# A fused attention, experts and gated layer: load order of q and k, the planner's durations, and the softmax factors spread before they are turned

## The chip, the cores and the metric

The kernel runs on one core of one Trainium2 chip. The metric is device time in microseconds (us); the time before is 1050.41 us, the median of three runs (1049.84 to 1050.56). The core's engines are TensorE (matrix products and transposes), VectorE, ScalarE, GpSimd, and SyncE, which issues most of the DMA transfers. Each runs its own instructions in order and waits for the others on semaphores.

## What is computed

The reference chains an attention, a mixture of experts and a gated layer, all in float32. The change lies in the attention (B, H, S, D = 4, 8, 576, 64):

```python
scores = scale * np.matmul(q, k.transpose(0, 1, 3, 2))
scores = np.where(causal, -1000000000.0, scores)
scores = scores - scores.max(-1, keepdims=True)
a = np.exp(scores)
a /= a.sum(-1, keepdims=True) + 1e-09
local = np.matmul(a, v)
# phi(x) = where(x > 0, x, exp(x) - 1) + 1
mem_out = np.einsum('bhsd,bhde->bhse', q_p, M_prev) / (np.einsum('bhsd,bhd->bhs', q_p, z_prev)[..., None] + 1e-06)
g = 1.0 / (1.0 + np.exp(-beta))[None, :, None, None]
return (g * mem_out + (1 - g) * local).astype(np.float32)
```

Here q_p is phi(q). The result, 2304 tokens of 512 numbers, goes through eight experts (each token to its best one) and then through `(sigmoid(x @ w_gate) * (x @ w_val)) @ w_out`.

## The kernel before

The attention works on 16 pairs of heads; a group is two pairs, so there are eight groups. For a group, SyncE loads q and k (`load_nat`, L230) in two halves l = 0, 1 of two heads each: two DMAs of 128 KB, and one of 32 KB for the last 64 rows. `load_z` (L246) loads z copied to all partitions in six DMAs, `load_M` (L262) M in two, `load_v` (L270) v in five. A pair's first three blocks of q and k need one half, its last two blocks both.

A pair then goes through these steps. TensorE turns q and k (`turn`, L322); ScalarE copies the high part of each and VectorE the low part (`q_part`, `z_part`, `k_part`); TensorE multiplies (`scores`, L391); VectorE adds the mask and finds each row's extreme (`masked`, L411); ScalarE takes the exponential and sums the rows (`exp`, L434); TensorE turns the probabilities (`turn_probs`, L475), ScalarE or VectorE keeps them (`keep_probs`), and TensorE multiplies with v (`out_part`, L504). GpSimd computes phi in four passes and a scaling (`phi_sum`, L286; `phi_scale`, L307), with the reduction between them on VectorE (`phi_norm`, L299). VectorE scales the product and adds the memory's part (`out_scale`, L519; `out_add`, L526).

The product with v comes out with the tokens along the free dimension, so a row's factor, (1 - g) over its sum, must be turned too and stand 64 times below itself. Before, `recip` (L441) makes nine factors per partition on VectorE, splits each into a high and a low part and writes these 18 columns into a table of 128 x 128; `rc_turn` (L451) transposes the table on TensorE, `rc_copy` (L455) brings it to SBUF, and `fan` (L458) multiplies it with six selection matrices of zeros and ones (`choices`, L210), four times for 128 columns and twice for the last 64; `fan_copy` (L471) takes the result to `rb`.

The order of all this is the work of a planner, `Plan` (L57). Each step has a rank, a cost in us for each engine that may do it, the steps that it needs and the buffers that it takes. `Plan.order` runs a list of ready steps forward in time by these costs and by a lag from engine to engine, and the program is written in the order found. The steps of the attention are entered in `Attention.run` (L533): `("L", "q", gi, l)` is a half of q, `("phs", gi, n)` a pass of phi, `("r", pi)` the factors, `("rt", pi)` and `("rk", pi)` their transposition and copy, `("b", pi, bk)` and `("bc", pi, bk)` the two parts of `fan` and `fan_copy`. The hardware then runs each engine's instructions in that order, whatever they take.

Of the kernel before, what the change touches and what calls it, by code (L numbers as in the profile page):

```python
# [56 lines left out]
class Plan:  # L57
# [7 lines left out]
    LAG = {"PE": 0.2, "SP": 2.2, "PL": 0.15, "DV": 0.2, "AC": 0.17, "Q": 0.0}  # L65
    SAME = {"PE": 0.0, "DV": 0.13, "PL": 0.1, "AC": 0.06, "SP": 0.0, "Q": 0.0}
# [16 lines left out]
    def order(self):  # L83
# [17 lines left out]
        while ready:  # L101
            best = None
            for n in ready:
# [4 lines left out]
                for e, c in cost.items():  # L108
                    t = max([free.get(e, 0.0), *t0, *(end[m][0] + (self.SAME if end[m][1] == e and (e != "SP" or n[0] == "ld") else self.LAG)[end[m][1]] for m in needs)])
# [24 lines left out]
class Attention:  # L134
# [14 lines left out]
    def constants(self, beta):  # L149
# [5 lines left out]
        self.rcs = [cp.tile([P, P], F32, name=f"rc{i}") for i in range(2)]  # L155
        self.rT = cp.tile([P, P], F32R, name="rT")
# [32 lines left out]
        for c in range(4):  # L189
            nc.vector.tensor_copy(self.iog[:, :, 2 * c : 2 * c + 2], o2)  # L190
        for j in range(2):
            r = slice(j * 64, (j + 1) * 64)
            nc.vector.tensor_copy(self.iog[r, :, 8:9], o2[r, :, j : j + 1])
# [16 lines left out]
    def choices(self):  # L210

        nc, cp, n = self.nc, self.cp, 2 * NQ
        whole = self.pt[1].rearrange("p h k q -> p (h k q)")[:, 0 : 6 * P].rearrange("p (c m) -> p c m", m=P)
        nc.gpsimd.memset(whole, 0.0)
        f = whole[0:n]
        fill = dict(compare_op=ALU.not_equal, fill=1.0, channel_multiplier=1)
        for part in range(2):
            for c in range(4):
                v = f[:, c].rearrange("p (j d) -> p j d", j=2)
                nc.gpsimd.affine_select(out=v, in_=v, pattern=[[-1, 2], [0, 64]], base=-NQ * part - 2 * c, **fill)  # L220
            for j in range(2):
                v = f[:, 4 + j, j * 64 : (j + 1) * 64]
                nc.gpsimd.affine_select(out=v, in_=v, pattern=[[0, 64]], base=-NQ * part - 8, **fill)
        self.pick = cp.tile([P, 6, P], F32R, name="pick")
        nc.gpsimd.tensor_copy(self.pick, whole)
        for rc in self.rcs:
            nc.gpsimd.memset(rc, 0.0)


    def load_nat(self, gi, nm, l):  # L230
# [6 lines left out]
        for hh in (2 * l, 2 * l + 1):  # L237
            self.nc.sync.dma_start(
                out=tv[:, :, hh, :], in_=src[b, h0 + hh, 0:512, :].rearrange("(c p) d -> p c d", p=P)
            )  # L240
        self.nc.sync.dma_start(
# [192 lines left out]
    def exp(self, pi, n):  # L434
# [3 lines left out]
            accum_out=self.sums[pi][:, n : n + 1],  # L438
# [12 lines left out]
    def rc_turn(self, pi):  # L451
        self.TR[pi] = T = self.ps_t.tile([P, 512], F32, name="T", tag="T")
        self.nc.tensor.transpose(T[:, 0:P], self.rcs[pi % 2], self.ident)

    def rc_copy(self, eng, pi):  # L455
        self.copy(eng, self.rT, self.TR[pi][:, 0:P])

    def fan(self, pi, bk):  # L458

        self.TR[pi, bk] = T = self.ps_t.tile([P, 512], F32, name="T", tag="T")  # L460
        r = self.rT
# [71 lines left out]
    def run(self, ex, change):  # L533
# [13 lines left out]
        def ac(n):  # L547
            return 0.06 + n / 1200
# [1176 lines left out]
```

## Time and profile before

| what | value |
|---|---|
| median of three runs | 1050.41 us |
| profiled execution | 1047.03 us |
| its span in the trace | 1045.3 us |
| TensorE (PE), busy share of the span | 95% |
| TensorE weight loads (PEld) | 82% |
| VectorE (DVE) | 52% |
| ScalarE (ACT) | 44% |
| GpSimd (POOL) | 21% |
| mean DMA rate | 100 GB/s |

The attention ends at about 270 us of the span, the experts' first product starts at 287.7, and the rest belongs to the experts and the gated layer. A share over the whole span says little about the attention, so its stretches have to be asked for apart. In the rows below a name such as `Sp<-kz,qT` is output and inputs, L399 a line of the kernel, x12 a count of instructions that are merged into one row, and the bracket gives how long the engine stood idle before and what ended it. SPq is SyncE's DMA queue, an issue's time is that of the issuing instruction and not of the transfer. Instructions of TensorE overlap in the array, so the distance from one start to the next is what counts there.

### The profile page before, as it was taken

To read this page: it belongs to the slowest core of one execution; us is meant where nothing else is said; L and a number is where in the kernel's file an instruction comes from. 1 tells how busy PE (TensorE), PEld (TensorE's weight loads), DVE (VectorE), ACT (ScalarE), POOL (GpSimd) and SP (SyncE) were. 2 spreads that over 40 slices of the span, in tenths; PEclk is the share of its full clock that TensorE was granted. 3 is DMA by queue.
4 is the path that set the end of the run, shared out by engine and by line. 5 is a ranking of instruction groups with operands and counts; after the bars stand their busy time and mean duration, and the time that the engine had idled before them with its cause. 6 is when DMAs were issued, how large, how long until landed. Compare 5 with 4: busy or idle time off the path is not lost. (4 is left out here: it accounts for less than half of the span.)

```text
span 1045.3 us, 18514 instructions
## 1 busy us (share of the span) xinstructions
PE 997.2 (95%) x5868; PEld 858.8 (82%) x5868; DVE 544.5 (52%) x1324; ACT 454.8 (44%) x1046; POOL 214.3 (21%) x344
## 2 busy tenths in 40 slices
PE   3989999899799999999999999999999999999997
PEld 3667777777688788888888999998999999999996
DVE  5897876777683853394466699912121121121111
ACT  3978786777542632282254555412221221122111
POOL 8785565332221111011011000001100100000001
PEclk9999999999999999999999999999999999999999
DMA  6756545430292661195247565300100100100000
GB/s 126 126 115 178 112 85 126 92 89 22 71 364 74 224 218 62 52 310 159 68 152 254 165 203 174 106 1 31 61 2 1 61 1 1 61 1 11 21 1 31
DMA packets 114851, 104.76 MB, mean 100 GB/s; under 512 B 71664, under 2 KB 89072, under 8 KB 114736
## 3 DMA queue, kind: packets, MB, share of 16 engines
q1 hardware_dynamic: 111264, 92.11, 30.9%
q0 software_dynamic: 3472, 11.30, 3.3%
q8 instruction: 49, 0.80, 0.3%
q14 instruction: 66, 0.54, 0.2%
HBM read 87.89 MB, written 15.50 MB: 99 GB/s over the span
## 5 line engine op out<-in xcount | busy, mean ns | idle before, releaser
L1532 DVE TENSOR_TENSOR G<-G,pT 128x384 f32<-128x384 f32 (+1 forms) x74 | 40.1, 542 | 247.6 <-PE pT L1518 239.6
L1564 POOL DMA_INDIRECT out_dram<-yo,rows x18 | 17.8, 991 | 453.5 <-ACT yo L1560 362.2
L1539 ACT ACTIVATE Gh<-G 128x384 fp32r<-128x384 f32 (+1 forms) x74 | 38.1, 516 | 158.2 <-DVE G L1532 158.0
L1313 PE MATMUL pY<-W,xh 128*128 128x512 f32 x368 | 98.0, 398 | 0.1
L1292 PE MATMUL pH<-W,xh 128*128 128x512 f32 x368 | 96.5, 394 | 0.7 <-ACT xh L1240 0.7
L1528 ACT ACTIVATE G<-pH 128x384 f32<-128x384 f32 x72 | 35.4, 491 | 121.0 <-PE pH L1518 120.6
L436 ACT ACTIVATE Sm<-Sm,mx 128x512 f32<-128x512 f32 (+3 forms) x144 | 83.6, 585 | 8.7 <-DVE mx L428 8.4
L1292 PEld LDWEIGHTS pH<-W,xh 128*128 128x128 f32 x368 | 69.6, 189 | 16.4 <-ACT xh L1240 1.0
L1313 PEld LDWEIGHTS pY<-W,xh 128*128 128x128 f32 x368 | 67.1, 188 | 13.5 <-ACT xh L1306 0.6
L1190 DVE TENSOR_TENSOR W<-raw,W 128x1024 fp32r<-128x1024 f32 x60 | 71.2, 1217 | 4.5 <-ACT W L1183 3.9
L428 DVE CUSTOM_DVE_ANT_0 Sm<-Sp,mask 128x512 f32<-128x512 f32 (+3 forms) x144 | 64.7, 482 | 15.9 <-PE T L480 6.9
L1306 ACT ACTIVATE xh<-pT 128x512 fp32r<-128x512 f32 x46 | 27.5, 598 | 101.9 <-PE pT L1232 91.8
L480 PE MATMUL T<-ident,Sm 128*128 128x128 f32 x400 | 62.2, 284 | 8.0 <-DVE xT L524 2.7
L1297 DVE TENSOR_SCALAR h<-pH 128x512 f32<-128x512 f32 x46 | 31.6, 687 | 72.0 <-PE pH L1292 71.1
L318 ACT ACTIVATE pt<-T 128x512 f32<-128x512 f32 (+4 forms) x138 | 56.0, 446 | 29.2 <-PE T L480 27.9
L480 PEld LDWEIGHTS T<-ident,Sm 128*128 128x128 f32 x400 | 44.8, 143 | 21.3 <-DVE xT L524 4.4
L1183 ACT ACTIVATE W<-raw 128x1024 fp32r<-128x1024 f32 x60 | 59.4, 1053 | 3.4 <-DVE xT L524 2.9
L1537 DVE TENSOR_TENSOR Gl<-G,Gh 128x384 fp32r<-128x384 f32 (+1 forms) x74 | 40.4, 545 | 32.7 <-ACT Gh L1539 32.7
L1292 PE MATMUL pH<-W,xl 128*128 128x512 f32 x184 | 56.3, 408 | 0.0
L1277 POOL DMA_INDIRECT xn<-x_dram,kept x23 | 25.5, 1110 | 149.2 <-DVEq L1359 86.4
L1313 PE MATMUL pY<-W,xl 128*128 128x512 f32 x184 | 49.9, 393 | 1.3 <-DVE xl L1304 1.3
L1304 DVE TENSOR_TENSOR xl<-pT,xh 128x512 fp32r<-128x512 f32 x46 | 31.7, 688 | 36.6 <-ACT xh L1306 30.7
(358 smaller groups left out, 2244.9 us busy)
## 6 DMA issues: line engine op xcount, KB each, us to landing
raw<-in_moe_w_dram SPq DMA_DIRECT2D x68, 512.0 KB, 5.9
y_dram<-y SPq DMA_DIRECT2D x23, 256.5 KB, 3.5
vn<-in_v_dram SPq DMA_DIRECT2D x40, 128.0 KB, 2.8
raw<-in_moe_w_gate_dram SPq DMA_DIRECT2D x10, 512.0 KB, 3.7
raw<-in_moe_w_val_dram SPq DMA_DIRECT2D x10, 512.0 KB, 3.8
raw<-in_moe_w_out_dram SPq DMA_DIRECT2D x10, 512.0 KB, 3.6
qn<-in_q_dram SPq DMA_DIRECT2D x32, 128.0 KB, 2.9
kn<-in_k_dram SPq DMA_DIRECT2D x32, 128.0 KB, 3.1
```

The lines of the kernel that those rows point to most:

```text
L318: self.nc.scalar.activation(out, in_, AF.Copy)
L428: self.nc.vector.tensor_tensor_reduce(out=self.Sm[pi, n][:, k0:k1], in0=self.Sp[pi, c][:, j if n < 8 else si, 0 : k1 - k0], in1=mask, scal ...
L436: self.nc.scalar.activation(self.Sm[pi, n], self.Sm[pi, n], AF.Exp, scale=-1.0, bias=self.mx[pi, n][:, si : si + 1], accum_out=self.sums[p ...
L480: nc.tensor.transpose(T[:, o * 128 : (o + 1) * 128], self.Sm[pi, n][:, k0 : k0 + 128], self.ident)
L1183: self.nc.scalar.activation(self.hi_lo(n)[0], self.first[n] if n in self.first else self.raw[n], AF.Copy)
L1190: eng.tensor_tensor(lo[:, o : o + w], t[:, o : o + w], hi.bitcast(F32)[:, o : o + w], ALU.subtract)
L1292: nc.tensor.matmul(pH[n], lhsT=a[:, m % 4, :], rhs=self.W1[:, c : c + 512], start=(m == 0), stop=(m == 11))
L1313: nc.tensor.matmul(pY[s % 2], lhsT=a[n][:, k * P : (k + 1) * P], rhs=self.W2[:, c : c + 512], start=(n == 0 and m == 0), stop=(n == 1 and ...
L1528: nc.scalar.activation(G[g, f][0], pp[g, f, 0], AF.Sigmoid)
L1532: nc.vector.tensor_tensor(t, t, p, ALU.mult)
L1537: nc.vector.tensor_tensor(l, t, hi.bitcast(F32), ALU.subtract)
L1539: nc.scalar.activation(hi, t, AF.Copy)
```

## The change

Four things change in the attention; the experts and the gated layer stay as they are.

1. Loads. `z`, `M` and `v` get later ranks, so both halves of q stand ahead of them. The first group's k is issued by ScalarE's own queue (a new engine name `AQ` in the planner), and its issues stand in ScalarE's program. The two small loads of the gate weights move from `Routing.constants` into a step of their own behind the first v.
2. Durations. The planner's costs for SyncE's issues, GpSimd's passes of phi and a few others are replaced.
3. Factors. `recip` keeps the nine factors, without a split, and makes two more columns of the first of them (the last 64 tokens, one column for each head of the pair). `spread` writes each of ten columns 64 times side by side into a tile of 128 x 640, on ScalarE or VectorE as the planner finds. `fan` transposes four blocks of it on TensorE, and multiplies the fifth with `fold`, two identity matrices one below the other, which adds its two halves.
4. The selection matrices, the table and its copy go, and their steps with them.

```diff
-    LAG = {"PE": 0.2, "SP": 2.2, "PL": 0.15, "DV": 0.2, "AC": 0.17, "Q": 0.0}
+    LAG = {"PE": 0.2, "SP": 2.2, "PL": 0.15, "DV": 0.2, "AC": 0.17, "AQ": 2.2, "Q": 0.0}
...
+        self.wides = [cp.tile([P, 5 * P], F32, name=f"wide{i}") for i in range(2)]
+        self.fold = cp.tile([P, 64], F32, name="fold")
+        nc.vector.tensor_tensor(self.fold, self.ident[:, 0:64], self.ident[:, 64:128], ALU.add)
+        self.head = cp.tile([P, 2], F32, name="head")
...
-    def load_nat(self, gi, nm, l):
+    def load_nat(self, eng, gi, nm, l):
+        queue = self.nc.scalar if eng == "AQ" else self.nc.sync
...
-        rc = self.rcs[pi % 2]
-        t = self.sp.tile([P, NQ], F32, name="rs", tag="rs", bufs=2)
-        nc.vector.scalar_tensor_tensor(t, self.sums[pi], 1e-9, self.iog[:, hp], ALU.add, ALU.mult)
-        nc.vector.reciprocal(t, t)
-        nc.vector.tensor_copy(rc.bitcast(F32R)[:, 0:NQ], t)
-        nc.vector.tensor_tensor(rc[:, NQ : 2 * NQ], t, rc[:, 0:NQ], ALU.subtract)
-
-    def rc_turn(self, pi):
...
+        self.rs[pi] = t = self.sp.tile([P, NQ + 2], F32, name="rs", tag="rs", bufs=2)
+        nc.vector.scalar_tensor_tensor(t[:, 0:NQ], self.sums[pi], 1e-9, self.iog[:, hp], ALU.add, ALU.mult)
+        nc.vector.reciprocal(t[:, 0:NQ], t[:, 0:NQ])
+        nc.vector.tensor_scalar(t[:, NQ:], self.head, t[:, 0:1], None, ALU.mult)
+
+    def spread(self, eng, pi):
+
+        self.wide[pi] = w = self.wides[pi % 2]
+        n = NQ + 1
+        self.copy(eng, w.rearrange("p (n d) -> p n d", d=64), self.rs[pi][:, 1:, None].to_broadcast([P, n, 64]))
...
         for n in range(3) if bk == 0 else (3,):
             o = (n - 3 * bk) * P
-            self.nc.tensor.matmul(T[:, o : o + P], lhsT=self.pick[:, n], rhs=r, start=True, stop=True, skip_group_check=True)
-        for j in range(2 * bk):
+            self.nc.tensor.transpose(T[:, o : o + P], w[:, n * P : (n + 1) * P], self.ident)
+        if bk:
             self.nc.tensor.matmul(
-                T[:, P : P + 64], lhsT=self.pick[:, 4 + j], rhs=r[:, j * 64 : (j + 1) * 64],
-                start=(j == 0), stop=(j == 1), skip_group_check=True,
+                T[:, P : P + 64], lhsT=w[:, 4 * P :], rhs=self.fold, start=True, stop=True, skip_group_check=True
             )
...
-                    add(("L", nm, gi, l), r + 2 * l + i, {"SP": 1.6}, lambda e, a=(gi, nm, l): self.load_nat(*a),
+                    add(("L", nm, gi, l), r + 2 * l + i, {"AQ" if (gi, nm) == (0, "k") else "SP": 1.9}, lambda e, a=(gi, nm, l): self.load_nat(e, *a),
...
-            add(("L", "z", gi), r + 2, {"SP": 2.7}, lambda e, g=gi: self.load_z(g), takes=[("zf", gi)])
+            add(("L", "z", gi), r + 3.5, {"SP": 3.3}, lambda e, g=gi: self.load_z(g), takes=[("zf", gi)])
...
-            for n, c in enumerate((3.06, 3.06, 2.57, 2.57)):
+            for n, c in enumerate((3.6, 3.6, 3.06, 3.06)):
```

What the planner makes of it, at three places. The first is the start on SyncE and on ScalarE (`qn`, `kn`, `zf`, `MB`, `vn` are the tiles of q, k, z, M and v; `wg` the gate weights). SyncE before:

```order
L238 DMA qn<-in_q_dram 128x4x64 x2
L241 DMA qn<-in_q_dram 64x2x64
L238 DMA kn<-in_k_dram 128x4x64 x2
L241 DMA kn<-in_k_dram 64x2x64
L251 DMA zf<-in_z_prev_dram 128x256 x4
L253 DMA zf<-in_z_prev_dram 64x128 x2
L238 DMA qn<-in_q_dram 128x4x64 x2
L241 DMA qn<-in_q_dram 64x2x64
L265 DMA MB<-in_M_prev_dram 64x2x64 x2
L747 DMA wg<-in_moe_w_gate_dram 128x4x8
L748 DMA wg<-in_moe_w_output_gate_dram 128x4x8
L238 DMA kn<-in_k_dram 128x4x64 x2
```

SyncE now; the last three rows belong to the second group:

```order
L224 DMA qn<-in_q_dram 128x4x64 x2
L227 DMA qn<-in_q_dram 64x2x64
L224 DMA qn<-in_q_dram 128x4x64 x2
L227 DMA qn<-in_q_dram 64x2x64
L237 DMA zf<-in_z_prev_dram 128x256 x4
L239 DMA zf<-in_z_prev_dram 64x128 x2
L251 DMA MB<-in_M_prev_dram 64x2x64 x2
L260 DMA vn<-in_v_dram 128x4x64 x4
L263 DMA vn<-in_v_dram 128x4x64
L224 DMA qn<-in_q_dram 128x4x64 x2
L227 DMA qn<-in_q_dram 64x2x64
L224 DMA kn<-in_k_dram 128x4x64 x2
```

ScalarE now, where k's issues surround the table load and the exponential of beta (`bt`):

```order
L224 DMA kn<-in_k_dram 128x4x64 x2
L227 DMA kn<-in_k_dram 64x2x64
L224 DMA kn<-in_k_dram 128x4x64
L186 ACT_TABLE_LOAD
L186 ACTIVATE bt<-bt 128x8
L224 DMA kn<-in_k_dram 128x4x64
L227 DMA kn<-in_k_dram 64x2x64
L340 ACTIVATE qT_117<-T 128x384
L362 ACTIVATE kz<-T 128x384
L270 ACTIVATE e<-qn 128x1152
```

The second half of q moved ahead of z, all of the first k moved to the other queue, and the second group's q moved behind v. The second place is VectorE at the factors of the ninth pair (`rs` the factors, `rc` the table, `rb` the turned factors). Before:

```order
L320 CAST rT<-T 128x128
L320 COPY rb<-T 128x192
L374 TENSOR_TENSOR kz<-T,kz 128x384
L446 SCALAR_TENSOR_TENSOR rs<-sums,iog 128x9
L447 RECIPROCAL rs<-rs 128x9
L448 CAST rc_109<-rs 128x9
L449 TENSOR_TENSOR rc_109<-rs,rc_109 128x9
L524 TENSOR_TENSOR xT<-O,rb 128x384
```

and now:

```order
L431 SCALAR_TENSOR_TENSOR rs<-sums,iog 128x9
L432 RECIPROCAL rs<-rs 128x9
L433 TENSOR_SCALAR rs<-head,rs 128x2
L306 COPY pt_159<-T 64x2x64
L306 COPY wide_109<-rs 128x640
L414 ISA Sm,mx<-Sp,mask 128x384
```

The two small operations and the copy of the turned table are gone, and the 640 columns of `wide` stand ahead of the next masked maximum. The third is TensorE at the factors of the last pair but one. Before:

```order
L406 MATMUL Sp<-kz,z_115 128x288 x6
L480 MATMUL T<-ident,Sm 128x128 x7
L453 MATMUL T<-ident,rc_109 128x128
L464 MATMUL T<-rT,pick 128x128 x4
L466 MATMUL T<-rT,pick 128x64 x2
L514 MATMUL O<-pt_154,vn 64x384 x2
```

and now:

```order
L447 MATMUL T<-ident,wide_109 128x128 x3
L316 MATMUL T<-ident,ph 128x128 x4
L320 MATMUL T<-ident,ph 128x128
L462 MATMUL T<-ident,Sm 128x128 x3
L392 MATMUL Sp<-kz,z_120 128x288 x6
L462 MATMUL T<-ident,Sm 128x128 x3
L447 MATMUL T<-ident,wide_109 128x128
L449 MATMUL T<-fold,wide_109 128x64
```

The first three blocks of the factors moved ahead of the last pair's last score products, and no table is turned before them.

## Rows read from the trace of the kernel before

**Rows 1.** Stretch; busy us of PE, PEld, DVE, ACT, POOL; granted clock, DMA share, GB/s.
```profile
0.00:270.50 270.50, 238.58 (x1955) 182.41 (x1959) 200.13 (x731) 198.09 (x628) 148.93 (x246) 0.99 0.49 104
35.00:40.00 5.00, 4.40 (x35) 3.61 (x35) 4.51 (x20) 5.00 (x18) 5.00 (x8) 1.00 0.81 68
180.00:190.00 10.00, 8.09 (x55) 6.38 (x51) 7.39 (x26) 6.37 (x21) 5.05 (x8) 0.83 0.42 52
```

**Rows 2.** Timeline of SyncE's DMA issues: start us, us, queue, line, operation.
```profile
0.74 0.98 SPq L238 DMA_DIRECT2D qn<-in_q_dram  x2
...
4.39 2.02 SPq L251 DMA_DIRECT2D zf<-in_z_prev_dram  x4
...
7.63 1.14 SPq L238 DMA_DIRECT2D qn<-in_q_dram  x2
...
10.43 2.61 SPq L265 DMA_DIRECT2D MB<-in_M_prev_dram  x2
...
14.87 1.05 SPq L238 DMA_DIRECT2D kn<-in_k_dram  x2
15.97 0.61 SPq L241 DMA_DIRECT2D kn<-in_k_dram  x1
...
19.45 1.05 SPq L238 DMA_DIRECT2D qn<-in_q_dram  x2
```

**Rows 3.** Timeline of TensorE, first 34 us; in brackets idle before and its end.
```profile
15.84 0.45 PE L334 MATMUL T<-ident,qn 128*128 128x128 f32 x1 [9.01 <-DMA qn<-in_q_dram]
...
18.51 0.48 PE L334 MATMUL T<-ident,kn 128*128 128x128 f32 x1 [0.95 <-DMA kn<-in_k_dram]
...
19.99 2.09 PE L399 MATMUL Sp<-kz,qT 64*128 64x512 f32 x12
...
26.48 0.49 PE L330 MATMUL T<-ident,qn 128*128 128x128 f32 x3
```

**Rows 4.** DMA issues of the first 30 us: count, KB each, median us to landing.
```profile
zf<-in_z_prev_dram SPq DMA_DIRECT2D x4, 128.0 KB, 6.1
```

**Rows 5.** Waits of SyncE's queue, first 60 us: us in total, times, longest.
```profile
SPq L265 <- DMA zf<-in_z_prev_dram: 2.3, 2, 1.4
```

**Rows 6.** Waits of the whole run: us in total, times, longest.
```profile
DVE nm L302 <- POOL e L297: 4.0, 2, 2.6
```

**Rows 7.** Timeline of ScalarE, first 34 us.
```profile
4.34 0.21 ACT L181 ACTIVATE bt<-bt 128x8 f32<-128x8 f32 x1 [2.32 <-DMA bt<-in_beta_dram]
```

**Rows 8.** Timeline of TensorE around one pair's factors.
```profile
44.16 0.77 PE L480 MATMUL T<-ident,Sm 128*128 128x128 f32 x5
44.68 0.64 PE L464 MATMUL T<-rT,pick 128*128 128x128 f32 x4
...
45.44 1.84 PE L514 MATMUL O<-pt,vn 128*64 128x384 f32 x16
```

**Rows 9.** Timeline of TensorE: f32 products of the logits.
```profile
271.94 1.18 PE L890 MATMUL T<-sel,LT 128*128 128x16 f32 x10
```

**Rows 10.** One line's instructions: ns min/median/max, first and last start, forms.
```profile
L446 DVE SCALAR_TENSOR_TENSOR rs<-sums,iog x16: 158/172/2410, 29.7 to 259.7; 128x9 f32<-128x9 f32 x16
```

**Rows 11.** VectorE's groups by shape, from 290 to 577 us: busy us, mean ns.
```profile
L1209 DVE TENSOR_SCALAR cv_a<-cv_a 128x512 f32<-128x512 f32 x6 | 2.5, 423 | 0.8 <-DVEq L1382 0.8
```

**Rows 12.** Timeline from 64.5 us: GpSimd, VectorE and TensorE.
```profile
65.13 3.06 POOL L297 TENSOR_TENSOR e<-ph,zf 128x320 f32<-128x320 f32 x4
...
65.80 2.41 DVE L446 SCALAR_TENSOR_TENSOR rs<-sums,iog 128x9 f32<-128x9 f32 x1
...
69.51 0.33 PE L480 MATMUL T<-ident,Sm 128*128 128x128 f32 x1 [1.09 <-DVE xT L524]
```

**Rows 13.** Timeline from 178 us: VectorE and TensorE.
```profile
182.54 1.35 DVE L302 TENSOR_REDUCE nm<-e 128x18 f32<-128x1152 f32 x1 [1.37 <-POOL e L297]
...
185.23 0.30 PE L330 MATMUL T<-ident,ph 128*128 128x128 f32 x1 [1.91 <-DVE xT L530]
...
185.70 1.91 PE L480 MATMUL T<-ident,Sm 128*128 128x128 f32 x8
```

More of the change, by code (lines that the diff above doesn't have):

```diff
@@ L108, in order @@
                 for e, c in cost.items():
-                    t = max([free.get(e, 0.0), *t0, *(end[m][0] + (self.SAME if end[m][1] == e and (e != "SP" or n[0] == "ld") else self.LAG)[end[m][1]] for m in needs)])
+                    t = max([free.get(e, 0.0), *t0, *(end[m][0] + (self.SAME if end[m][1] == e and (e != "SP" or n[0] in ("ld", "L")) else self.LAG)[end[m][1]] for m in needs)])
                     b_ = self.later.get(e, 0.0) if len(cost) > 1 else 0.0
@@ L637, in run @@
             r = u0 + 20
-            add(("r", pi), r, {"DV": 0.7}, lambda e, a=pi: self.recip(a), needs=[("e", pi, n) for n in range(NQ)] + ["pick"],
+            add(("r", pi), r, {"DV": 0.55}, lambda e, a=pi: self.recip(a), needs=[("e", pi, n) for n in range(NQ)],
                 takes=[("rc", pi)], uses=[("sums", pi)])
-            add(("rt", pi), r, {"PE": 0.15}, lambda e, a=pi: self.rc_turn(a), needs=[("r", pi)], takes=[("T", ("rt", pi))], uses=[("rc", pi)])
-            add(("rk", pi), r, {"AC": ac(128), "DV": dv(128)}, lambda e, a=pi: self.rc_copy(e, a), needs=[("rt", pi)], takes=[("rT", pi)], uses=[("T", ("rt", pi))])
+            add(("rw", pi), r, {"AC": ac(5 * P), "DV": dv(5 * P)}, lambda e, a=pi: self.spread(e, a), needs=[("r", pi)], takes=[("wd", pi)], uses=[("rc", pi)])
             for bk in range(2):
                 r, n = u0 + 21 + bk, QB[bk][1] - QB[bk][0]
-                add(("b", pi, bk), r, {"PE": PO + 0.33}, lambda e, a=(pi, bk): self.fan(*a), needs=[("rk", pi), "pick"] + ([("b", pi, 0)] if bk else []),
-                    takes=[("T", ("b", pi, bk))], uses=[("rT", pi)])
+                add(("b", pi, bk), r, {"PE": PO + (0.22 if bk else 0.3)}, lambda e, a=(pi, bk): self.fan(*a), needs=[("rw", pi)] + ([("b", pi, 0)] if bk else []),
+                    takes=[("T", ("b", pi, bk))], uses=[("wd", pi)])
                 add(("bc", pi, bk), r, {"AC": ac(n), "DV": dv(n)}, lambda e, a=(pi, bk): self.fan_copy(e, *a),
@@ L681, in run @@
             add(("k", n), 15 + n, {"PL": c}, lambda e: next(steps), needs=[("k", n - 1)] * (n > 0))
+        add("wg", 20, {"SP": 0.9}, lambda e: self.routing.load_gates(), needs=[("k", 0), ("L", "v", 0)])
         for b in range(B):
             self.routing.plan(self, add, b)
-        wide = [n for n in p.steps if n[0] in ("phn", "qh", "ql", "zh", "zl", "S", "m", "r", "rt", "rk", "b", "bc", "t", "v", "o", "os")]
+        wide = [n for n in p.steps if n[0] in ("phn", "qh", "ql", "zh", "zl", "S", "m", "r", "b", "bc", "t", "v", "o", "os")]
         for n in range(8):
@@ L803, in constants, with load_gates @@
         yield
+    def load_gates(self):
+        for i, w in enumerate(self.w_gates):
+            self.nc.sync.dma_start(out=self.wg[:, :, i * 8 : i * 8 + 8], in_=w.rearrange("(k p) e -> p k e", p=P))
     def cols(self, b):
@@ L813, in plan @@
         for bk in range(2):
-            add(("lg", b, bk), r, {"PE": 0.6}, lambda e, a=(at, b, bk): self.logits(*a), needs=xs[bk::2] + ([("lg", b, 0)] if bk else [("k", 4)]),
+            add(("lg", b, bk), r, {"PE": 0.6}, lambda e, a=(at, b, bk): self.logits(*a), needs=xs[bk::2] + ([("lg", b, 0)] if bk else [("k", 4), "wg"]),
                 takes=[("T", ("lg", b, bk))], uses=[("xT", b)], mode=3)
```

60 lines of the change are left out of this document (18 added, 42 removed).

## The prediction

> **What bounds the kernel now.** I read the busy time by stretch first, since the program is three stages in a row. The attention fills the first 270.5 us, and TensorE is busy 238.58 us of them [rows 1]; behind it come the experts and the gated layer, which the diff does not touch. So the change is worth what it takes off the attention, where TensorE does nothing for about 32 us. Where these lie is the next question. The DMA issues and the first uses show the largest piece: SyncE issues the first half of q and of k, then z, then the second half of q, and the second half of k only at 14.87 us [rows 2]. TensorE waits 9.01 us for the second half of q, until 15.84, and again for k until 18.51, and the first score products start at 19.99 [rows 3]. z is what holds the queue up: each of its large transfers takes 6.1 us to land, where the second k half is there 18.51 - 16.58 = 1.9 us after its last issue ended (15.97 + 0.61), and SyncE waits for z before it can issue M [rows 2 to 5]. Next come the engines behind the scores: from 35 to 40 us ScalarE is busy 5.00 of 5 us and VectorE 4.51 [rows 1], so the ramp is theirs rather than TensorE's. The last views are the waits and the timeline around a later gap. There VectorE, which runs in program order, stands before a reduction that needs GpSimd's product, twice in all, 4.0 us together [rows 6]; behind it are the additions that free accumulators.
>
> **The start: q and k before z, k on ScalarE's queue.** A half of q or k is three issues, and the second k half took SyncE 16.58 - 14.87 = 1.7 us for them [rows 2]. Two halves of q back to back, from 0.74, end at 4.2. On ScalarE four of k's six issues go out by about 3.0 at the same rate; then come the table load and the exponential of beta, which ended at 4.55 before [rows 7], and behind it the last two k issues, to about 5.7. That ScalarE waits for beta there delays nothing else, since its first copy needs a transposed q. With 1.9 us to landing k is whole at 7.6. But z is now issued from 4.2 on the other queue, beside k's last two transfers, and z's own 6.1 us is the other end: 5.7 + 6.1 = 11.8. I take 9.5, nearer the low end because only two of the six transfers meet z. From k's arrival to the first scores it took 19.99 - 18.51 = 1.5 us; now the second q half's exponential and the first blocks of the second pair stand in between, so I take 2.2. **Scores then start at 11.7 instead of 19.99: 8.3 us earlier** (10.2 at the low end, 6.0 at the high end).
>
> A rule of the Trainium skill speaks against the second queue. "DMA: Bandwidth & Descriptors", section "Issuing engines are not separate DMA queues", says that DMAs started by different engines run on the same sixteen DMA engines and interleave, and that a second issuer only saves issue time. No row here has a transfer that ScalarE started. On one queue the four halves would be issued by 0.74 + 4 x 1.7 = 7.5 and landed by 9.5, the value taken above, so by that rule the order of the loads is worth the 8.3 and the queue nothing.
>
> Who is late next: the loads of the second group. SyncE issued its first q at 19.45, and TensorE used it at 26.48 [rows 2, 3], 6.5 us after the first scores. Now z, M and v stand ahead of it. z's six issues take 3.2 us (4.39 to 7.63), so they end at 7.4 and z has landed at 13.5; M and v are held by it as M was, whose two issues took 2.6 us, and some 2 us of both lie behind that. So the issue comes at about 15.5, only 4 us earlier than before, and has landed 1.7 + 1.9 later, at 19.1. TensorE would be there at 11.7 + 6.5 = 18.2. I charge 1.0, and 0 to 3.5 as bounds (nothing, if ScalarE is behind by then anyway; the whole difference between 8.3 and 4 us with what hangs on it). **Term A: -8.3 + 1.0 = -7.3 us** (-10.2 to -2.5). The gate weights go behind v; they are first read by the logits, far later. GpSimd no longer builds the selection matrices; phi is first transposed long after the first scores, so I cost this at 0. If its chain came late, the pairs' last additions would wait, not the scores.
>
> **The softmax factors on TensorE.** Per pair it did one transpose of the factor table, four products against selection matrices and two more for the last 64 columns. From the first product to the next work is 45.44 - 44.68 = 0.76 us, and a transpose is (44.68 - 44.16) / 5 = 0.104, so 0.86 in all [rows 8]. Now it does four transposes, 0.42, and one product in full f32 with 64 columns. The nearest row to that is the logits' f32 product with 16 columns, ten instructions in 1.18 us, two to a product: 0.24 [rows 9]. So 0.66 us, and **term B is 16 x (0.66 - 0.86) = -3.2 us**. Ends: -3.6; and with 0.12 for a transpose and 0.36 for the product 16 x (0.84 - 0.86) = -0.3. It counts nearly in full, as TensorE is the busy engine after the ramp.
>
> **The same on VectorE and ScalarE.** Of the chain's small nine-column operations, 0.17 us in the median [rows 10], two go (cast and subtraction) and one comes (the last block's two columns); the copy of the turned table goes, eight times on each engine. What comes is the spread: 640 columns from SBUF to SBUF, twelve times on VectorE and four on ScalarE in the new order. The nearest row is a 512-column VectorE operation from SBUF to SBUF, 423 ns [rows 11], so 0.53 for 640; as the other end 1.1, as the spread reads each input 64 times and no row shows such a read. New on VectorE is 12 x 0.53 + 16 x 0.17 = 9.1 us, and 32 x 0.17 = 5.4 and eight copies go: near 0 in sum. But the spread is one long piece in VectorE's order, and masked maxima that TensorE needs queue behind it. On the other side the chain has two engine changes less. I charge **term D: +1.0 us** (-1 to +4).
>
> **Measured durations in the planner.** It sorts all steps by estimated times. GpSimd's product of phi with z was entered at 2.57 us; four pieces of it take 3.06 [rows 12]. So VectorE's reduction stood too early: at 182.54 VectorE had waited 1.37 us for GpSimd, TensorE stood idle for 1.91 until 185.23, and then eight transposes took 1.91 us, 0.24 each instead of 0.104 [rows 8, 13]; the granted clock of that stretch is 0.83 [rows 1], so part of it ran at 1.2 GHz. That is 1.9 + 8 x 0.136 = 3.0 us and some more until the clock was back, say 3.8. The other such wait, of 2.6 us, falls into the ramp, where ScalarE has a queue; I count 1. If the order now places the reductions right, 4.8 us go. SyncE's costs rise too, which moves prefetches that have slack. But a new order also makes collisions that the old trace can't show, so I take half: **term C: -2.4 us** (-4.8 to 0).
>
> **Sum.** -7.3 - 3.2 + 1.0 - 2.4 = -11.9 us on the profiled execution's own 1047.03 (span 1045.3 and 1.7 around it): 1035.1. The median of the runs shown is 1050.41, 3.4 above that execution, so the forecast is 1050.4 - 11.9 = **1038.5 us**.
>
> **Rivals.** First, the gain is given back in the ramp: the late loads and the full ScalarE hold the scores, so that half of A stays, and the new order misses as often as the old (C = 0): -3.6 - 3.2 + 1.0 = -5.8, 1044.6. For it: ScalarE's 5.00 of 5 us and SyncE's waits for z. Against it: ScalarE's queue there is filled by what TensorE gives it, which all comes earlier. Second, everything goes right, A without the late loads, all of C, no charge for the spread: -8.3 - 3.6 - 4.8 = -16.7, 1033.7. Third, k's last transfers are shuffled among z's packets and land at 11.8, scores at 14.0: A is -6.0 + 1.0 = -5.0, the rest as forecast, 1040.8. Fourth, on the **slower side**, VectorE's spread and GpSimd shut each other out. The timeline from 64.5 us has such a case: a nine-column operation of VectorE with both inputs in SBUF took 2.41 us while GpSimd's product ran, and TensorE then waited 1.09 us [rows 12]. Held like that at 1.09 us, all twelve spreads cost 13.1 us; where each also drops the clock as at 182 us, 3.8 each. It decides from eleven of twelve at 1.09, or from four at 3.8 (11.9 / 3.8 = 3.1); six at 3.8 give 22.8 - 11.9 = +10.9, 1061. For it: GpSimd is busy 148.93 of the 270.5 us [rows 1]. Against it: the median of that nine-column operation is 0.17, so 2.41 is rare [rows 10]. The Trainium skill's "SBUF — State Buffer", section "Who interferes with whom", has the rule: an operation that needs the port pair which VectorE and GpSimd share waits until the other's instruction is over, and an f32 copy between SBUF tiles can be one. The trace agrees for the form with two SBUF inputs; no row shows a copy of this size beside GpSimd. That the change does nothing is ruled out by the order, as q's second half now stands ahead of z.
>
> **How the numbers follow.** Forecast 0.52 (its own range 1035 to 1042), given back 0.22, all goes right 0.13, k shuffled 0.07, VectorE held 0.06. 1032 to 1045 leaves out the slower case, nearly half of the first rival and a little of the second, together under 0.2. About 2 us, 0.2%, is what a measurement of this kernel can tell from no change. A fifth of the first rival comes that close to the old time, and a little of the last one: faster 0.90, same 0.05, slower 0.05.
>
> **What would show it.** The first score product at 11 to 13 us in the new timeline bears out the start; at 14 or later, with TensorE waiting for k, the shuffling. A wait for q before the second group's first transposes shows the late load. Four transposes and one product in 0.66 us bear out B. No wait of VectorE's reduction for GpSimd and no dip of the granted clock near 180 us bear out C. Spreads above 1.1 us on VectorE beside GpSimd's products would be the last rival. The prediction is wrong if the scores start early and the attention ends less than 5 us sooner.

## The result, and the profile after

The changed kernel takes **1036.24 us**, the median of four runs (1035.56 to 1037.3), against 1050.41. The ratio, estimated from the single runs, is 0.9869, with a 95% interval of 0.9852 to 0.9886 (the two medians alone give 0.9865). The forecast was 1038.5, and its range holds the time. How it comes about is another matter: two terms of the sum come near their size, one doesn't, one stays open, and a stall that no term named took back over half of what the changes had gained by then.

First the busy time by stretch of the changed kernel (columns as in rows 1), the same stretches as [rows 1] and then four more:

```profile
0.00:270.50 270.50, 245.10 (x2003) 190.45 (x2003) 209.54 (x757) 208.10 (x636) 146.02 (x231) 0.97 0.51 108
35.00:40.00 5.00, 5.00 (x46) 3.96 (x47) 4.37 (x19) 4.93 (x18) 5.00 (x7) 1.00 0.65 147
180.00:190.00 10.00, 9.90 (x87) 7.62 (x86) 7.63 (x30) 7.73 (x27) 0.31 (x1) 1.00 0.26 57
90.00:95.00 5.00, 2.63 (x20) 1.83 (x18) 4.01 (x16) 1.22 (x2) 4.32 (x6) 1.00 0.68 209
95.00:100.00 5.00, 1.91 (x10) 1.47 (x11) 1.30 (x4) 2.52 (x9) 5.00 (x7) 0.75 0.88 61
100.00:105.00 5.00, 3.62 (x18) 2.75 (x16) 4.96 (x12) 2.23 (x6) 5.00 (x7) 0.50 1.18 208
105.00:110.00 5.00, 4.80 (x22) 3.50 (x24) 4.37 (x15) 4.57 (x17) 1.42 (x3) 0.50 0.61 150
```

From 35 to 40 us TensorE is full now (5.00 of 5 us, 4.40 before), though from 30 to 35 it is emptier (3.32, 3.99 before), and the gap at 180 us is gone with its dip of the clock (9.90 of 10 busy at 1.00, against 8.09 at 0.83). But from 90 to 100 us TensorE does 4.54 us of work in 10, and then its granted clock is 0.50, the lower level of 1.2 GHz, for ten.

**The start.** ScalarE's timeline with its DMA queue (ACTq), then SyncE's and TensorE's, answer to [rows 2, 3 and 7]:

```profile
2.59 0.83 ACTq L224 DMA_DIRECT2D kn<-in_k_dram  x1
...
5.79 0.21 ACT L186 ACTIVATE bt<-bt 128x8 f32<-128x8 f32 x1 [1.05 <-DMA bt<-in_beta_dram]
5.80 0.37 ACTq L224 DMA_DIRECT2D kn<-in_k_dram  x1
6.21 0.62 ACTq L227 DMA_DIRECT2D kn<-in_k_dram  x1
```

```profile
5.50 2.24 SPq L237 DMA_DIRECT2D zf<-in_z_prev_dram  x4
...
17.47 1.06 SPq L224 DMA_DIRECT2D qn<-in_q_dram  x2
```

```profile
10.95 0.45 PE L320 MATMUL T<-ident,kn 128*128 128x128 f32 x1 [2.62 <-DMA kn<-in_k_dram]
...
12.61 0.79 PE L385 MATMUL Sp<-kz,qT 64*128 64x512 f32 x2
...
22.16 0.55 PE L316 MATMUL T<-ident,qn 128*128 128x128 f32 x3
```

k is whole at 10.95 us, the scores start at 12.61 instead of 19.99, and the second group's q is there when TensorE comes to it (no bracket at 22.16).

**The factors**, TensorE's timeline around the last pair (answers to [rows 8]):

```profile
254.09 0.60 PE L447 MATMUL T<-ident,wide 128*128 128x128 f32 x4
254.53 0.33 PE L449 MATMUL T<-fold,wide 128*128 128x64 f32 x2
254.79 0.54 PE L496 MATMUL O<-pt,vn 128*64 128x384 f32 x2
```

They take 254.79 - 254.09 = 0.70 us. The spread itself, one line's instructions (ns minimum, median, maximum), and VectorE's reduction with the waits before it (us in all, times):

```profile
L306 DVE COPY wide<-rs x12: 478/492/625, 25.5 to 211.5; 128x640 f32<-128x640 f32 x12
```

```profile
L288 DVE TENSOR_REDUCE nm<-e x8: 1342/1348/1353, 30.3 to 206.7; 128x18 f32<-128x1152 f32 x8
its engine sat idle before it (us, times) until:
  POOL e L283: 1.6, 1
```

**The new stall.** Timelines of SyncE, ScalarE, TensorE and VectorE from 90 us:

```profile
90.57 0.41 SPq L973 DMA_DIRECT2D x_dram<-xt  x1
91.08 1.92 SPq L237 DMA_DIRECT2D zf<-in_z_prev_dram  x4
...
94.41 3.98 SPq L973 DMA_DIRECT2D x_dram<-xt  x2
```

```profile
97.44 0.60 ACT L304 ACTIVATE xt<-T 128x512 f32<-128x512 f32 x1 [6.21 <-DMA x_dram<-xt]
...
104.55 0.60 ACT L304 ACTIVATE xt<-T 128x512 f32<-128x512 f32 x1 [2.74 <-DMA x_dram<-xt]
```

```profile
98.09 0.47 PE L316 MATMUL T<-ident,kn 128*128 128x128 f32 x1 [5.45 <-ACT xt L304]
...
105.20 1.11 PE L462 MATMUL T<-ident,Sm 128*128 128x128 f32 x4 [1.58 <-ACT xt L304]
```

```profile
101.78 4.67 DVE L431 SCALAR_TENSOR_TENSOR rs<-sums,iog 128x9 f32<-128x9 f32 x1
```

At the end of a batch row the result is turned and kept in tiles `xt` of 128 x 512 (two buffers, `x_keep`), which SyncE stores. The first store stands behind v, M and an expert's weights in SyncE's order and goes out at 90.57, 2.4 us after its copy; z follows it. ScalarE, in program order, waits for this store with the third tile's copy until 97.44, and everything behind that copy waits too. That z's transfers are what makes the store late to land is likely and was not tested.

One marker follows the lead over the kernel before: the product of the last 64 columns of a pair's factors, L466 before and L449 after. It comes 13.3 us earlier in the fourth pair (78.86 against 92.14), 4.9 us earlier in the fifth (106.96 against 111.84) and 11.1 us earlier in the last (254.53 against 265.65). So 8.4 us were lost in one place, and later gaps of the old order gave back 6.2. Of the 11.1 the experts' first product keeps 9.8 (276.59 against 286.34).

### The profile page after: what moved, and what is told of

Read it like the earlier page. It is cut to its first block, busy times and chain, and to the rows that moved or that the text cites. A ratio compares the mean times of both kernels' runs of the same rounds, so it can differ in the third digit from the quotient of the medians.

```text
span 1035.5 us, 18407 instructions
## 1 busy us (share of the span) xinstructions
PE 996.8 (96%) x5852; PEld 861.2 (83%) x5852; DVE 545.5 (53%) x1322; ACT 456.2 (44%) x1040; POOL 210.3 (20%) x322
## 5 line engine op out<-in xcount | busy, mean ns | idle before, releaser
L422 ACT ACTIVATE Sm<-Sm,mx 128x512 f32<-128x512 f32 (+2 forms) x144 | 83.6, 587 | 8.0 <-DVE mx L414 7.6
L414 DVE CUSTOM_DVE_ANT_0 Sm<-Sp,mask 128x512 f32<-128x512 f32 (+2 forms) x144 | 64.7, 483 | 8.6 <-PE Sp L392 3.0
L304 ACT ACTIVATE pt<-T 128x512 f32<-128x512 f32 (+4 forms) x130 | 53.5, 449 | 16.4 <-PE T L462 15.5
```

The source lines that it names most:

```text
L304: self.nc.scalar.activation(out, in_, AF.Copy)
L414: self.nc.vector.tensor_tensor_reduce(out=self.Sm[pi, n][:, k0:k1], in0=self.Sp[pi, c][:, j if n < 8 else si, 0 : k1 - k0], in1=mask, scal ...
L422: self.nc.scalar.activation(self.Sm[pi, n], self.Sm[pi, n], AF.Exp, scale=-1.0, bias=self.mx[pi, n][:, si : si + 1], accum_out=self.sums[p ...
```

## The experiments

Each experiment is compared with the kernel before on the same chip, which took 1048.5 to 1048.7 us in the four sets of experiments; the changed kernel's own comparison is the one with 1050.41. The ratios are estimated from the single runs, and the quotients of the medians differ from them by up to 0.14%.

| kernel | median us | ratio to before | 95% interval |
|---|---|---|---|
| changed kernel | 1036.24 | 0.9869 | 0.9852 to 0.9886 |
| third x tile | 1030.69 | 0.9817 | 0.9793 to 0.9842 |
| k on SyncE | 1039.15 | 0.9897 | 0.9874 to 0.9920 |
| spread twice | 1036.19 | 0.9876 | 0.9858 to 0.9894 |
| loads undone | 1043.28 | 0.9940 | 0.9921 to 0.9959 |
| durations undone | 1041.24 | 0.9930 | 0.9914 to 0.9947 |
| loads only | 1052.78 | 1.0043 | 1.0023 to 1.0063 |
| factors only | 1042.85 | 0.9954 | 0.9939 to 0.9969 |
| durations only | 1052.81 | 1.0038 | 1.0020 to 1.0056 |
| durations and third x tile | 1051.97 | 1.0032 | 1.0020 to 1.0045 |
| third x tile, k divided | 1028.35 | 0.9802 | 0.9788 to 0.9815 |
| the same, norm late | 1032.19 | 0.9842 | 0.9828 to 0.9856 |
| the same, norm behind corrections | 1029.13 | 0.9818 | 0.9804 to 0.9832 |

**A third buffer for the x tiles**, the order of all instructions unchanged:

```diff
-            xt = self.r2.tile([P, DM], F32, name="xt", tag="xt")
+            xt = self.r2.tile([P, DM], F32, name="xt", tag="xt", bufs=3)
```

> The changed kernel with a third buffer for the x tiles, in the same order of instructions on every engine (the planner still counts two). Theory: the changed kernel lost its lead at 92 to 107 us because ScalarE's copy of an x tile waited 6.2 and 2.7 us for the store of the tile two before, TensorE stood idle and its clock was granted at 0.5. The last product of the fifth pair's factors came at 78.86 in the fourth pair and 106.96 in the fifth; without the wait it comes at 98 to 99 and the whole takes 1036.2 - 8.5 = 1027.7 us, with no clock below 1.0 between 90 and 120 us. Rival: VectorE's small operation that GpSimd held for 4.67 us at 101.8, or the loads around it, would stop TensorE at the same place anyway: 1034 to 1036, with the clock falling there again.

0.9817. The stall is gone; ScalarE's timeline and the stretches of this kernel:

```profile
94.67 0.60 ACT L304 ACTIVATE xt<-T 128x512 f32<-128x512 f32 x1
...
99.61 0.60 ACT L304 ACTIVATE xt<-T 128x512 f32<-128x512 f32 x1
```

```profile
95.00:100.00 5.00, 3.56 (x29) 2.66 (x28) 4.83 (x16) 4.36 (x14) 5.00 (x7) 1.00 0.97 132
100.00:105.00 5.00, 4.82 (x47) 3.63 (x47) 4.86 (x20) 4.81 (x18) 5.00 (x7) 1.00 1.00 198
...
35.00:40.00 5.00, 4.54 (x27) 3.84 (x27) 3.87 (x16) 3.85 (x13) 5.00 (x7) 0.60 0.64 144
```

From the fourth pair's marker to the fifth's it takes 102.14 - 82.42 = 19.7 us, where the changed kernel took 28.1: the stall was worth 8.4 us, as expected. Of the four runs one took 1027.45, the time expected, and three took 1030.6 to 1031.3; the profiled one of these has the clock at 0.60 from 35 to 40 us, where the profile of the changed kernel, with the same waits at 33 us, had 1.00. At the fourth pair's marker this execution is 3.6 us behind that of the changed kernel (82.42 against 78.86), of which k, whole only at 11.89 us, makes 0.9. So the theory holds, and the 3 us lie ahead of the stall. The rival falls: VectorE's small operation takes 0.17 us here, at 100.78.

**k on SyncE's queue:**

```diff
-        queue = self.nc.scalar if eng == "AQ" else self.nc.sync
+        queue = self.nc.sync
```

> The changed kernel with the first group's k issued by SyncE between q and z, in place of ScalarE; nothing else is moved. Theory (only the place of the loads ahead of z counts, not the second queue): k is whole within 1 us of the 10.95 us that it has on ScalarE's queue, the first score product stands at 11.6 to 13.6 instead of 12.61, and the time is 1036.2 within 1 us. Rival (the second issuer is worth its issue time): four halves in a row end at about 9.3, k is whole at 12.5 to 13.5, the scores start near 14.5 and the time is 1038. A second rival: later z, v and second group hold the ramp: scores within 1 us but 1039 or more.

TensorE's timeline of this kernel:

```profile
9.79 0.47 PE L320 MATMUL T<-ident,kn 128*128 128x128 f32 x1 [1.09 <-DMA kn<-in_k_dram]
...
11.47 1.22 PE L385 MATMUL Sp<-kz,qT 64*128 64x512 f32 x4
...
22.53 0.52 PE L316 MATMUL T<-ident,qn 128*128 128x128 f32 x3 [1.44 <-DMA qn<-in_q_dram]
```

On one queue k is whole 1.16 us earlier than on two, since nothing there waits for beta. What the second queue buys is that z, M and v go out earlier (z at 5.50 us instead of 8.08): here the second group's q is late by 1.44 us. The second rival describes it best. But three of its runs took 1038.7 to 1039.7 and the fourth 1036.07, and the intervals of the two kernels overlap: that ScalarE's queue is worth time in the end is likely and not settled.

**The spread written twice:**

```diff
+        for _ in range(2):
             self.copy(eng, w.rearrange("p (n d) -> p n d", d=64), self.rs[pi][:, 1:, None].to_broadcast([P, n, 64]))
```

> The changed kernel with each spread of the factors written twice over (twelve more on VectorE, four on ScalarE), same order otherwise. Theory: the spread lies beside TensorE's work, so that 12 x 0.49 + 4 x 0.74 = 8.8 us more of it cost 0 to 2 us: 1036 to 1038. Rival: VectorE and ScalarE bound the attention together with TensorE, so that most of the 8.8 us comes out at the end: 1042 to 1045. If GpSimd holds the spread, single ones above 1.1 us show.

0.9876 against 0.9869: by the times, 8.8 us more of it cost 0.7 us, which the intervals don't tell from nothing, though they leave room for some 3. The number is the theory's, but the trace shows that part of the 8.8 us was paid and then hidden. TensorE's timeline at the fourth pair's marker, and ScalarE's at the third x tile:

```profile
81.08 0.33 PE L450 MATMUL T<-fold,wide 128*128 128x64 f32 x2
```

```profile
96.83 0.60 ACT L304 ACTIVATE xt<-T 128x512 f32<-128x512 f32 x1 [3.40 <-DMA x_dram<-xt]
```

With k as early as in the changed kernel (10.92 us) and the clock at 1.00 in both up to 90 us, the fourth pair's marker comes 2.2 us later (81.08 against 78.86). ScalarE's wait for the stored tile is then 2.8 us shorter (3.40 against 6.21), and the fifth pair's marker comes 0.8 us earlier than in the changed kernel (106.13 against 106.96); at the last pair it is still 0.7 us earlier. So from the fifth pair on the spread lies beside TensorE's work; in the first four pairs, where VectorE and ScalarE are nearly full, TensorE waits for it (1.19 us for VectorE at 64.60, where the changed kernel has 0.46 at 62.40), and the stall swallowed that. One execution of each kernel shows this.

**Parts undone, parts alone.** Two kernels take one part out of the changed kernel, three put one part alone into the kernel before. For the loads the edit is, forwards or backwards:

```diff
-add(("L", nm, gi, l), r + 2 * l + i, {"SP": 1.6},
+add(("L", nm, gi, l), r + 2 * l + i, {"AQ" if (gi, nm) == (0, "k") else "SP": 1.6},
-add(("L", "z", gi), r + 2,
+add(("L", "z", gi), r + 3.5,
-add(("L", "v", gi), r + 3,
+add(("L", "v", gi), r + 4,
```

with M ranked as v and the gate weights behind the first v. The planner's rule for a load's second half goes with the loads. For the durations it is the numbers of the diff (q and k 1.6 to 1.9, z 2.7 to 3.3, GpSimd's passes, the stores), for the factors the functions `recip`, `spread` and `fan` with their steps and costs. With the loads undone in the changed kernel, the gate weights stay in their own step.

> The changed kernel with the loads in their old order (z between the halves, k on SyncE), factors and durations kept. Theory: the first scores go back to 19 to 21 us, and as the start was worth 7.4 us the time is 1043 to 1044 if the order that follows also has a wait for a stored x tile near the second batch row; if that wait is gone with the other order, 7.4 - 8.5 or so: 1034 to 1037. Rival: the first 20 us are made up for in the ramp, as ScalarE is full there: 1036 with the wait, 1028 without.

> The changed kernel with the old durations of loads, stores and GpSimd's phi; factors and the order of the loads kept. Theory: the wait of 6.2 and 2.7 us for the stored x tile comes with the durations, so it goes (-8.4) and a wait for GpSimd's product comes back (+2 to +5): 1030 to 1033 us. Rival: the wait for the store comes with the earlier start, whatever the durations: 1038 to 1041.

> The kernel before with the new order of the loads alone (q and k first, k on ScalarE's queue, z, M, v and the gate weights later); factors and durations as before. Theory: the first score product stands at 12 to 13 us instead of 19.99, and most of that lasts: 5 to 8 us less than the kernel before. Rival: the ramp takes half of it back, 2 to 4 us less, with the lead over the kernel before falling between the first and the fourth pair.

> The kernel before with the new factors alone (spread and turned in place, no selection matrices); loads and durations as before. Theory by the prediction's terms: 16 x 0.16 to 0.20 us less on TensorE and about nothing on VectorE: 2 to 3 us less than the kernel before. Rival: it also takes the wait for the turned table out of the chain of a pair and so keeps TensorE busy in the ramp: 5 us less or more. A second rival: a new collision, as the order is another: 0 to 3 us more.

> The kernel before with the measured durations alone; loads and factors as before. Theory: VectorE's reduction no longer waits for GpSimd near 180 us, and the clock stays at 1.0 there: 2 to 5 us less than the kernel before. Rival: the lower cost of the x tile's store makes the order put the copies of x tiles close together, so that ScalarE waits several us for a store near the second batch row: no gain, or up to 6 us more.

Taken out of the changed kernel, the loads are worth 0.9940 - 0.9869 = 0.71%, 7.4 us, and the durations 0.61%, 6.4 us. Put alone into the kernel before, the loads cost 0.43% and the durations 0.38%; the factors gain 0.46%. Three parts that sum to a loss of some 3.7 us make a gain of 14 together. With the loads undone the wait for a stored tile is still there, so the time was to be 1043 to 1044, and is. With the durations undone that wait shrinks (ScalarE 1.69 us at 102.9), but others open, as TensorE's 2.58 us for VectorE at 50.7; the rival's 1038 to 1041 was the nearer number, though not for its reason. Beside the factors (0.9954) the loads bring 0.24% and the durations 0.14%, both near the noise, and the two together 0.85%. The lead over the kernel before at the fourth pair's marker says the same: 0.0 us with the factors alone, 3.3 with the loads alone, -1.0 with the durations alone, 3.6 with the durations undone, 6.7 with the loads undone, and 13.3 with all three.

The profiles show what happens with the parts alone. TensorE up to the last pair's marker, from its busy time in stretches of 5 us (idle is what is missing to 5; lost to the clock is the stretch times one minus the granted clock):

| kernel | marker at | idle, first 20 us | idle, later | lost to clock |
|---|---|---|---|---|
| before | 265.65 | 14.8 | 17.1 | 1.7 |
| loads only | 266.43 | 9.4 | 19.6 | 5.1 |
| factors only | 262.58 | 15.3 | 14.5 | 5.1 |
| durations only | 269.47 | 15.1 | 17.4 | 6.8 |
| loads undone | 259.95 | 13.8 | 13.1 | 3.4 |
| durations undone | 258.18 | 8.9 | 16.5 | 5.1 |
| changed | 254.53 | 8.8 | 14.1 | 6.8 |
| third x tile | 248.70 | 10.1 | 9.2 | 3.4 |
| third x tile, k divided | 246.92 | 7.4 | 9.4 | 3.4 |

The loads alone save 5.4 us in the first 20 and lose 2.5 us to later gaps and 3.4 to the clock. One place is the reduction of [rows 6], which the old durations still put too early; VectorE's and TensorE's timelines and the stretch behind, of the kernel with the loads only:

```profile
48.20 1.35 DVE L303 TENSOR_REDUCE nm<-e 128x18 f32<-128x1152 f32 x1 [1.00 <-POOL e L298]
```

```profile
50.79 0.33 PE L331 MATMUL T<-ident,kn 128*128 128x128 f32 x1 [2.10 <-DVE qT L353]
```

```profile
50.00:60.00 10.00, 9.11 (x51) 7.17 (x53) 8.45 (x36) 8.26 (x25) 9.59 (x12) 0.66 0.45 97
```

Two more places follow: TensorE waits 1.83 us at 88.4 for ScalarE's copy of the turned table, with the clock at 0.72 from 90 to 95, and 1.88 us at 110.5 for a masked maximum. The lead over the kernel before falls from 3.3 us at the fourth pair to -2.2 at the fifth.

```profile
88.37 0.66 PE L465 MATMUL T<-rT,pick 128*128 128x128 f32 x4 [1.83 <-ACT rT L319]
```

So the expected loss in the ramp is there, but larger than its rival had it. The early start needs the right durations, and, as the turned table's copy suggests, the new factors too; the loads and durations without the factors were not run. The durations alone do remove the wait for GpSimd, as expected, and run into the store of an x tile: TensorE waits at 176.93 for ScalarE's copy.

```profile
176.93 1.39 PE L480 MATMUL T<-ident,Sm 128*128 128x128 f32 x4 [3.47 <-ACT xt L318]
```

This was the rival for that kernel, and to see whether that wait is the loss, the third tile was tried there too, again in the same order:

> The kernel before with the measured durations and a third buffer for the x tiles, in the same order of instructions as the durations alone (1052.81 us, 1.0038 of the kernel before). Theory: the durations lose because ScalarE waits 3.4 us at 176 us for the store of an x tile, TensorE with it (3.47 us), and its granted clock falls behind that; without the wait 5 to 7 us less, 1046 to 1048 or 0.997 to 0.999 of the kernel before. Rival: the wait of 2.28 us for VectorE at 89.7 with the clock behind it is the dearer part: only 2 to 3 us less, 1.001 to 1.002.

1.0032: the theory falls, and the time is above the rival's 1.001 to 1.002 too. ScalarE's, SyncE's, VectorE's and TensorE's timelines of it:

```profile
173.56 0.57 ACT L318 ACTIVATE xt<-T 128x512 f32<-128x512 f32 x1
177.17 0.60 ACT L318 ACTIVATE xt<-T 128x512 f32<-128x512 f32 x1 [3.04 <-DMA x_dram<-xt]
```

```profile
171.24 1.22 SPq L238 DMA_DIRECT2D kn<-in_k_dram  x2
...
173.20 1.01 SPq L992 DMA_DIRECT2D x_dram<-xt  x2
```

```profile
86.44 3.58 DVE L446 SCALAR_TENSOR_TENSOR rs<-sums,iog 128x9 f32<-128x9 f32 x1
```

```profile
91.07 0.33 PE L453 MATMUL T<-ident,rc 128*128 128x128 f32 x1 [2.29 <-DVE pt L320]
```

The third copy no longer waits, but the fourth does, nearly as long as the third had (3.04 us against 3.37): tiles that were ready from 169.6 us on are stored at 173.20, behind q and k in SyncE's order. A buffer helps only where a store is issued soon. The other wait, 2.29 us behind an operation that GpSimd held, stays as it was, with the clock at 0.66 in the ten microseconds behind. Which of the two costs this kernel more is left open.

**Better versions.** The third tile, with the halves of the first k on different queues:

```diff
-        queue = self.nc.scalar if eng == "AQ" else self.nc.sync
+        queue = self.nc.scalar if eng == "AQ" and l == 0 else self.nc.sync
```

> The changed kernel with the third x tile of the first experiment and the first group's k divided: its first half on ScalarE's queue, its second on SyncE's behind q and ahead of z. Theory: ScalarE's last k issues were held by the wait for beta until 5.8 us; now k is whole at 8.5 to 9.8 instead of 10.95, the scores start at 10.5 to 11.5 instead of 12.61, z starts 0.7 us later than in the changed kernel and the second group's q is still in time: 0 to 2 us less than the kernel with the third x tile alone (ratio to the kernel before 0.980 to 0.982). Rival: the second group's q comes late as with all of k on SyncE (a wait of 1.4 us at 22.5) and takes it back: same or 1 us more.

**1028.35 us, 0.9802 (0.9788 to 0.9815)**: the fastest kernel of this study. TensorE's timeline:

```profile
8.34 0.47 PE L320 MATMUL T<-ident,kn 128*128 128x128 f32 x1 [0.50 <-DMA kn<-in_k_dram]
...
11.36 1.22 PE L385 MATMUL Sp<-kz,qT 64*128 64x512 f32 x4
...
32.09 1.49 PE L462 MATMUL T<-ident,Sm 128*128 128x128 f32 x8 [1.11 <-DVE kz L360]
```

k is whole at 8.34, the scores start at 11.36, and TensorE doesn't wait for the second group's q. Against the third tile alone (0.9817) the intervals overlap. What is left in the ramp is the wait at 32 us, where VectorE does the first group's norm of phi ahead of the corrections of q and k. Two kernels moved that norm by hand in the list of steps. The late one, written short:

```diff
+move([("phn", 0), ("ph", 0), ("phe", 1), ("phs", 1, 0)], behind=("m", 2, 7, 0))
+move([("X", "ph", 0, 0), ..., ("pp", 1, 1)], behind=("S", 2, 1))
```

> The kernel with the divided k, and beside it the first group's norm of phi (VectorE's reduction and three small operations, 2.0 us) moved by hand behind the masked maxima of the third pair's first scores, with what hangs on it (GpSimd's product, phi's transposes and their copies). Theory: TensorE's waits near 32 us (1.12 and 0.45 us, in some runs with the clock at 0.5 for 3 to 5 us behind them) come from VectorE doing this norm ahead of the corrections of q and k; without them 1.5 us less in each run and 3 us in those with the dip: ratio 0.976 to 0.979. Rival: the order behind the move makes TensorE wait for phi or GpSimd's next phi come late: no gain or 1 to 3 us more.

And behind the corrections:

```diff
+move([("phn", 0), ("ph", 0), ("phe", 1)], behind=("zl", 3))
```

> The kernel with the divided k, and the first group's norm of phi moved by hand behind the corrections of the fourth pair's q and k only, ahead of the masked maxima. Theory: TensorE's transposes near 32 us start 1 us earlier, but the maxima still come behind the norm, and TensorE's next scores wait for them: half of the gain of the later place, 0 to 1.5 us less than with the divided k alone. Rival: as large as with the later place, since the wait for the corrections was the one that counted.

Neither is faster: the late one is 0.4% slower than without the move, the other within the intervals. TensorE's timeline of the late one, then of the other:

```profile
36.88 0.62 PE L385 MATMUL Sp<-kz,qT 64*128 64x256 f32 x6 [1.64 <-DVE mx L414]
```

```profile
35.46 0.48 PE L447 MATMUL T<-ident,wide 128*128 128x128 f32 x1 [2.56 <-ACT pt L304]
```

In the late one the norm now stands ahead of maxima that TensorE needs as well; in the other ScalarE waits with the next group's exponential (which needs the buffer that the norm reads), and copies queue behind it. From 30 to 35 us VectorE is busy 4.85 of 5 in the changed kernel: at both places tried, the two microseconds moved within this full stretch are waited for.

## Why the prediction was right, and where not

**Term A (-7.3) came out at 7.4**, by undoing it in the changed kernel, give or take 2.7 by the intervals; the two profiled executions differ by 6.0 (1043.35 against 1037.30). But it is not the loads' own worth: alone they cost 0.43%, 4.5 us. That one term for them comes out so near is in part luck. Its parts were off against each other. k was whole at 10.95 instead of 9.5: the step "which ended at 4.55 before" failed, since beta, which ScalarE had at 4.34 before, let it go on only at 5.79, and the last two k issues went out at 5.80 and 6.21. So the scores stand at 12.61, 0.9 us later than said, and 7.4 us earlier than before instead of 8.3. The late second group (+1.0) did not happen: its q was issued at 17.47, even later than the 15.5 forecast, but had no wait. The bound of 3.5 for it was less than the difference that it names (8.3 - 4 = 4.3); nothing hung on that. The third rival, 14.0 us for the scores, did not occur. The Trainium skill's "DMA: Bandwidth & Descriptors", section "Issuing engines are not separate DMA queues", would have the second queue save issue time alone; here the trace agrees, and k even arrives earlier on one queue (9.79 against 10.95).

**Term B (-3.2)** is 16 x (0.70 - 0.86) = -2.6 by the same rows as in the forecast. With **term D (+1.0)** the factors were to bring 2.2; alone they bring 0.46%, 4.8 us, and 3.0 between the two profiled executions (1044.05 against 1047.03). Their marker has hardly a lead over the kernel before in the first six pairs (-1.3 to 0.6 us), and 3.1 us at the last. That fits a charge for the spread in the ramp and a gain on TensorE behind it. The spread takes 0.49 us (0.53 forecast); written twice, it cost 2.2 us up to the fourth pair and nothing from the fifth on. So D was the right kind of charge, and its size stays open, since no run has the new factors without a spread. What the rest of the 4.8 is, no run isolates.

**The fourth rival** had its mechanism right for the small operation and wrong for the spread. The nine-column operation with two inputs in SBUF took 4.67 us at 101.78, to the end of two of GpSimd's passes of phi, and 3.58 us in the kernel with the durations and the third x tile. Of the twelve spreads eight ran beside GpSimd, and none took over 0.63 us. The Trainium skill's "SBUF — State Buffer", section "Who interferes with whom", allows both forms to be shut out for an instruction; the trace agrees for the first (longer than one instruction, even) and shows 0.14 us at most for the second (0.625 against a median of 0.492).

**Term C (-2.4) is the step that failed.** What it named is right: the reduction waits for GpSimd once, 1.6 us, instead of twice with 4.0 in all [rows 6], and the gap and the dip at 180 us [rows 13] are gone. But its worth is not the sum of removed waits. Alone, the durations cost 4.0 us; beside the other two they bring 6.4, and that with the stall of 8.4 us at the x tiles already taken off. "A new order also makes collisions that the old trace can't show" was the right warning with too small a number, and one collision the old trace did show. This row of VectorE's timeline of the kernel before stands in no group, and I passed over it:

```profile
175.16 0.69 DVE L320 COPY xt<-T 128x512 f32<-128x512 f32 x1 [1.60 <-DMA x_dram<-xt]
```

It is the same wait for a stored x tile, harmless there since TensorE has no gap behind it. Six copies wait so in the kernel before, 5.3 us in all, and behind two of them TensorE waits itself, 0.82 us at 108.65 and

```profile
237.22 0.66 PE L480 MATMUL T<-ident,Sm 128*128 128x128 f32 x4 [0.98 <-ACT xt L318]
```

The change lowers the planner's cost of that store from 0.75 to 0.6 us. No run changes this cost alone, and with the old costs the wait can grow as well: with the factors alone TensorE waits 1.98 us for an x tile at 170.78.

**The sum** was right by luck, because two errors cancelled. By the fourth pair the lead was 13.3 us, where the terms that apply there give some 8 to 9 (A, a quarter of B and D, the early part of C); then 8.4 were lost at the x tiles. The test at the end of the forecast, that the attention ends at least 5 us sooner, was met with 11.1.

## What to carry to other kernels

A planner's order is a whole: parts that gain together may lose alone, and a sum of removed waits says little where every change makes a new order. Search the old trace for small waits that hit an engine with slack, above all for a buffer that a store still reads, since the next order may put them on the busy engine. And test a suspected stall with the order held fixed, by a buffer more, which told here in one line what a newly planned order would have blurred. A test by added work needs the trace as well: a stall further on can swallow what the work cost, and the time then shows nothing.

## What the runs showed of the hardware

The runs of one program differ, in part with TensorE's clock. With the same order and the same waits of 1.1 and 0.45 us near 33 us (the changed kernel and the one with the third x tile), the granted clock from 35 to 40 us stayed at 1.00 in one profile and fell to 0.60 in the other; the changed kernel's four runs split into 1035.6 and 1035.7 us at a mean clock of 0.990 and 1036.7 and 1037.3 at 0.987. Nine of ten runs of the durations alone took 1050.7 to 1054.7 us at 0.987 or 0.988; the tenth had 0.994 and took 1046.0. The clock is not all of it: two runs with the third x tile took 1031.3 us at 0.992 and 1027.5 at 0.993.

A copy on VectorE that reads each element 64 times, 640 columns from SBUF to SBUF, takes 0.49 us, in line with the plain row of [rows 11]; on ScalarE it takes 0.74.
